# Ten instead of nine of the sixteen inner chunks in the first phase of a planned three-layer kernel

## The chip, the cores and the metric

One core of one Trainium2 chip runs the whole program. The metric is the device time of one execution in microseconds (us), as the median of several runs. The engines are PE (TensorE, the matmuls), DVE (VectorE), ACT (ScalarE), POOL (GpSimd) and SP (SyncE, which here issues all DMAs, the transposing ones too). Each engine takes its instructions strictly in the order in which they were written.

## The reference

Three layers follow each other: causal attention with a decay, a feed-forward layer with 2,048 inner features, and a second one with 1,024 inner features, a softmax gate and a layer norm.

```
# q, k, v: [4, 8, 576, 64], f: [4, 8, 576]
cum = cumsum(log(clip(f, 1e-4, 1)))
scores = q @ k.T / 8 + cum[:, None] - cum[None, :], causal
attn = softmax(scores) @ v                      # -> x: [2304, 512]
h = x @ w_in;  g = max(0.01 * h, h);  x = g @ w_out          # w_in [512, 2048]
h = x @ w2_in                                               # w2_in [512, 1024]
solu = h * softmax(h);  ln = layernorm(solu) * g_ln
out = ln @ w2_out                                           # [2304, 512]
```

## The kernel before

Every number is kept as a high and a low part (a split into two fp32r or fp16 tiles), so that each product takes three matmuls: high by high, high by low, low by high.

**Attention** goes by pairs of heads: 4 pairs for each of the 4 batches (`pair`). The first batch is done in two rounds, blocks 0 and 1 of all four pairs first, then blocks 2, 3 and 4; the other batches take whole pairs. A pair loads q and k into a `raw` tile (two of them), splits it into `kq` tiles on ACT, DVE and POOL, makes scores into `ps_s` (four PSUM banks), a softmax on ACT and DVE, a transposing DMA (`pt<-hl`), and the product with v into `ps_v` (one bank). Its result is spilled to DRAM (`xs_d`).

**The first feed-forward layer** goes by 9 blocks of 256 tokens. Its 16 chunks of 128 inner features are divided between two phases by the constant `FA`. In the first phase `ffn_a` does chunks 0 to `FA`-1 of every block: `load_x` fetches the block through two `xw` tiles into split `x` tiles, `hidden` makes a chunk (12 matmuls `ps_f<-x,wi`, two ACT and one DVE instruction into `g`), and `y_mms` adds up the output (12 matmuls `ps_f<-g,wo` a chunk); four partial outputs leave through `yo` tiles to DRAM (`yp_d`). These matmuls are woven into attention: blocks 0 and 1 can go when the first batch is spilled, blocks 2 and 3 after the second, 4 and 5 after the third. In the second phase `ffn_b` does the rest of the chunks (with `wib` and `wob`), adds the stored part, and `layer2` and `layer2_out` do the last layer.

**Weights** pass through `weight`: a load of 512 KB into a staging tile, a copy of the high halves into a `wk` tile (ACT or POOL), one DVE instruction (L798), a copy to the high part and a subtract into the low part. Up to `WI0` chunks of `wi` and `WO0` of `wo` are staged in three `wst` tiles, later ones in the two `raw` tiles that attention's loads use as well.

**Space** sets an order too. The tiles of the pool `early` (`wst`, `qa`, `vre`) lie where the pool `main` (`x`, `xw`, `g`, `yo`) comes later. So nothing of `main` can be written before the last weight that is staged in `wst` is done. The load of `glt` in `main` marks this place in SP's row.

**Order** is set by a planner (`Plan`): each operation has a priority and guessed durations, the planner plays a run through and writes out the instructions of each engine in the order that it finds. A changed count of operations or tiles so moves much else. `heirs` hands a tile on to another name when its first name needs it no more.

Of the kernel before, what the change touches and what calls it, by code (L numbers as in the profile page):

```python
# [7 lines left out]
F32 = mybir.dt.float32  # L8
# [4 lines left out]
BF16 = mybir.dt.bfloat16  # L13
AF = mybir.ActivationFunctionType
ALU = mybir.AluOpType
AX = mybir.AxisListType

B, H, S, D = 4, 8, 576, 64
# [3 lines left out]
KD = DM // 128  # L22
NC = DFF // 128
NC2 = DF2 // 128
FA = 9
PT = 4
NVT = 4
NWST = 3
NE = 2
EARLY = 1779.78  # L30
WI0 = 9
WO0 = 8
WLATE = 66.27
NVE = 1
# [23 lines left out]
TB = 256  # L58
# [271 lines left out]
def dve(n):  # L330
    return 1.042 * n + 70
# [18 lines left out]
def mmr(n):  # L350
    return n / 2.4 + 2.5 if n > 255 else 80.0
# [6 lines left out]
def body(tc, kqa, kq, vt, f, wa, w2i, w2o, gln, out):  # L358
    nc = tc.nc
    es = ExitStack()  # L360
    P = Plan()
# [3 lines left out]
    base = es.enter_context(tc.tile_pool(name="base", bufs=1))  # L365
# [3 lines left out]
    def tiles(pool, name, n, shape, dt):  # L369
        return [pool.tile(shape, dt, name=f"{name}{i}") for i in range(n)]  # L370


    P.tag("wi", tiles(base, "wi", FA, [128, 2, 512], F32R))
    P.tag("wo", tiles(base, "wo", FA, [128, 2, 512], F32R))
    P.tag("raw", tiles(base, "raw", 2, [128, KQ], F32))
    P.tag("wk", tiles(base, "wk", 2, [128, 512], I32))
    glt = base.tile([128, NC2], F32, name="glt")
    halfm = base.tile([128, 1], F32, name="halfm")
# [6 lines left out]
    ap = attn.enter_context(tc.tile_pool(name="attn", bufs=1))  # L385
# [1 line left out]
    P.tag("VT", tiles(ap, "VT", NVT, [128, 5, 2, 2, 64], F16))  # L387
    P.tag("u", tiles(ap, "u", 5, [128, 1], F32))
    P.tag("vs", tiles(ap, "vs", 2, [128, 4], I32))
    P.tag("sd", tiles(ap, "sd", 3, [128, S + 2], F32))  # L390
    P.tag("st", tiles(ap, "st", 6, [128, 12], F32))
    P.tag("hl", tiles(ap, "hl", 3, [128, 1536], F16))
    P.tag("pt", tiles(ap, "pt", PT, [128, 12, 128], F16))
    P.tag("xr", tiles(ap, "xr", 2, [128, S], F32))
    ident = ap.tile([128, 128], F32R, name="ident")
    P.tag("va", tiles(ap, "va", 2, [128, 1], F32R))
    mask = ap.tile([128, 512], BF16, name="mask")
    mask4 = ap.tile([128, S], BF16, name="mask4")
    zcol = ap.tile([32, 1], F32, name="zcol")
    zrow = zcol.to_broadcast([32, S])  # L400
    P.tag("qk", [tuple(ap.tile([128, KQ], F32R, name=f"kq{n}_{j}") for j in range(2)) for n in range(NQK)])
# [13 lines left out]
    def heirs(old, *plan):  # L415
        P.tags.setdefault(old, Tag(old)).heirs.extend(plan)
        for nm in plan:
            if not callable(nm):
                P.tags.setdefault(nm, Tag(nm))


    def copy_on(eng, o, i, scale=None):
# [50 lines left out]
    def setup():  # L473
        nc.gpsimd.memset(qa[64:66, 0], 1.0)
        nc.vector.memset(qa[64:66, 1], 1.0)
        nc.vector.memset(mask, 0.0)
        one_at = P.tags["sd"].free[-1][:, 0:128]
        nc.vector.memset(one_at, 0.0)
        nc.gpsimd.affine_select(
            one_at, one_at, pattern=[[-1, 128]], compare_op=ALU.not_equal, fill=1.0, base=0, channel_multiplier=1)  # L480
        nc.vector.tensor_copy(ident, one_at)
        nc.vector.memset(mask4, 0.0)
        nc.gpsimd.affine_select(
            mask[:, 384:512], mask[:, 384:512], pattern=[[-1, 128]], compare_op=ALU.is_ge,
            fill=NEG, base=0, channel_multiplier=1)
        for o in (0, 64):
            nc.gpsimd.affine_select(
                mask4[o:o + 64, 512:576], mask4[o:o + 64, 512:576], pattern=[[-1, 64]],
                compare_op=ALU.is_ge, fill=NEG, base=0, channel_multiplier=1)
        nc.gpsimd.memset(halfm, -0.5)  # L490
        for k in P.tags["wk"].free:
            nc.gpsimd.memset(k, 0)
        nc.vector.memset(zcol, 0.0)
# [131 lines left out]
    def qk_mm(Q, full, i, o, hd, k0, k1, first, last):  # L625
        _, qk, col = Q
        c0 = col[i]
        if full:
            a = qk(hd)
            mm(o, a[0:66, c0:c0 + 128], a[0:66, k0:k1], first, last)  # L630
            return
        a, b = qk(hd)
        mm(o, a[:, c0:c0 + 128], a[:, k0:k1], first, False)
        mm(o, b[0:68, c0:c0 + 128], b[0:68, k0:k1], False, last)
# [40 lines left out]
    def scores(p, unit, hd, prio, full):  # L675

        sts, parts, n, at = P.buf("st"), [], 0, 0
        for j, i in enumerate(unit):
            W = 128 * (i + 1)
            joint = i < 2 and len(unit) > 1  # L680
            if i == 1 and joint:
                at = 128
            else:
                ps, at = P.buf("ps_s"), 0
            view = lambda at=at, W=W, ps=ps: ps.t[:, at:at + W]
            key = (ps, j) if joint else ps
            P.op(PE, 4 * W / 2.4 if full else 2 * mmr(W), lambda Q=QK[p], i=i, W=W, view=view: qk_mm(
                Q, full, i, view(), hd, 0, W, True, True), prio, r=QK[p][0][hd], heat=HEAT if full else 1.0,
                **({"rw": [ps]} if at else {"w": [ps]}))
            parts.append([view, sts, j, W, [(n, n + W, 0, W)], key, i])  # L690
            n += 2 * W
        for view, _, j, W, _, key, i in parts:
            P.op(DVE, dve(W) + 130, lambda i=i, j=j, view=view: nc.vector.tensor_tensor_reduce(  # L693
                view(), view(), mask[:, 384 - 128 * i:512], -0.125, 3.0e38, ALU.add, ALU.min, sts.t[:, j:j + 1]),
                prio, w=[(sts, j)], rw=[key])
        parts = [x[:6] for x in parts]
        pt = softmax(parts, prio)
        return {i: (pt, x[4][0][0] // 128) for i, x in zip(unit, parts)}

    def scores4(p, prio, full):  # L700

        pa, pb, sts = P.buf("ps_s"), P.buf("ps_s"), P.buf("st")
        bq = QK[p][0]
        parts = []
        for ps, k0, k1, init in ((pa, 0, 512, 3.0e38), (pb, 512, S, None)):
            def pe(ps=ps, k0=k0, k1=k1, Q=QK[p]):
                for hd in range(2):
                    qk_mm(Q, full, 4, ps.t[:, 0:k1 - k0], hd, k0, k1, hd == 0, hd == 1)

            n = k1 - k0  # L710
            P.op(PE, 8 * n / 2.4 if full else 4 * mmr(n), pe, prio, w=[ps], r=bq[0] + bq[1], heat=HEAT if full else 1.0)
            P.op(DVE, dve(n) + 130, lambda ps=ps, k0=k0, k1=k1, n=n, init=init: nc.vector.tensor_tensor_reduce(
                ps.t[:, 0:n], ps.t[:, 0:n], mask4[:, k0:k1], -0.125, sts.t[:, 1:2] if init is None else init,
                ALU.add, ALU.min, sts.t[:, 0:1] if init is None else sts.t[:, 1:2]),
                prio, r=[(sts, 1)] if init is None else [], rw=[ps],
                w=[(sts, 0) if init is None else (sts, 1)])
            parts.append((lambda ps=ps, n=n: ps.t[:, 0:n], sts, 0, n,
                          [(0, 512, 0, 512)] if k0 == 0 else [(1024, 1088, 0, 64)], ps))
        return softmax(parts, prio)
# [125 lines left out]
    def y_mms(o, c, d, g, n, first, last):  # L845
        w = WO[c].t
        wh, wl = (w[:, j, 128 * d:128 * d + 128] for j in range(2))
        gh, gl = (g.t[:, j, 0:n] for j in range(2))
        mm(o, wh, gh, first, False)
        mm(o, wh, gl, False, False)  # L850
        mm(o, wl, gh, False, last)
# [23 lines left out]
    def ffn_a(blk, prio):  # L875
        eprio = prio - EP
        xb = load_x(blk, prio, "x")
        gs = [hidden(c, xb, TB, "ps_f", "g", prio + c, eprio + c) for c in range(FA)]
        YPD[blk] = []
        for d in range(KD):  # L880
            ps, yo = P.buf("ps_f"), P.buf("yo")
            for q in range(2):
                cs = range(FA // 2 * q, FA if q else FA // 2)

                def pe(cs=cs, d=d, ps=ps):
                    for c in cs:
                        y_mms(ps.t[:, 0:TB], c, d, gs[c], TB, c == 0, c == FA - 1)

# [5 lines left out]
    def ffn_b(tb, prio):  # L894
# [9 lines left out]
        at = [lambda: p01.t[:, 0:TB], lambda: p01.t[:, 512:512 + TB], lambda: p2.t[:, 0:TB], lambda: p3.t[:, 0:TB]]  # L904
        for c in range(FA, NC):
            g = hidden(c, xb, TB, "ps_g", "g2", prio + 2 * (c - FA), eprio + c)
# [100 lines left out]
    with tc.manual_schedule():  # L1007
# [6 lines left out]
        for p in range(KD):  # L1014
            pair(p, PB + PB0 * p, (2, 3, 4))
        for load_w, t, n, at in ((load_wi, "wi", WI0, WIP), (load_wo, "wo", WO0, WOP)):
            for c in range(FA):
# [6 lines left out]
        def main():  # L1024
            early.close()
            nc.sync.dma_start(glt, gln)
            mp = es.enter_context(tc.tile_pool(name="main", bufs=1, side="right"))
            P.tag("x", tiles(mp, "x", 8, [128, 2, TB], F32R))
            P.tag("xw", tiles(mp, "xw", 2, [128, 2, TB], F32))
            P.tag("g", tiles(mp, "g", FA, [128, 2, TB], F32R))  # L1030
            P.tag("yo", tiles(mp, "yo", 4, [128, TB], F32))

        P.op(CTL, 1.0, main, 0.0, deps=[o for o in P.ops if any(b.tag.name in ("wst", "qa", "vre") for b in o.bufs)])
        for blk in range(NB):
# [28 lines left out]
        for n in ("ps_f", "ps_g", "yo", "wst", "raw", "raw2", "wk"):  # L1063
            P.tags.setdefault(n, Tag(n)).fifo = False
        heirs("py01", "ph")
        heirs("raw", "raw2", "raw2")
        heirs("x", *(["x2"] * 4 + ["ln"] * 4))
        heirs("g", *(["g2"] * (FA - 5) + ["y2"] * 5))
        heirs("ps_f", "ps_g", "ps_g", "py3")
# [56 lines left out]
```

## Time and profile before

| what | value |
|---|---|
| median of 3 runs (lowest, highest) | 850.28 us (850.12, 850.7) |
| the profiled execution | 849.04 us |
| its span, first to last instruction | 847.2 us |
| mean granted TensorE clock | 0.98 |
| PE busy | 777.7 us (92%) |
| PE weight loads busy | 707.1 us (83%) |
| DVE, ACT, POOL busy | 523.0, 488.8, 364.5 us |

The shares are means over stages of different kinds: up to 98 us PE does attention alone, up to about 368 us attention with feed-forward matmuls between, and afterwards feed-forward work alone. The profiled execution lies 1.84 us over its span, and 1.24 us under the median.

### The profile page before, as it was taken

Reading aid. Unit: us, or ns where it says so; the run is one execution under the profiler, and the core shown is the slowest. Engines: PE = TensorE matmul, PEld = TensorE weight load, DVE = VectorE, ACT = ScalarE, POOL = GpSimd, SP = SyncE. Lnnn points to the kernel's source line nnn. Section 1 sums busy time; section 2 is a strip of 40 time slices with the busy share of each in tenths; the row PEclk is TensorE's granted clock in tenths of the full one; section 3 lists DMA queues with packets and bytes.
Section 4 is the critical chain, followed back from the end, with each engine's and each line's share of the span. In section 5 each row is a group of like instructions: output and inputs, shape, how many; then the busy total and the mean of one; then the engine's idle time right before and its main releaser. Section 6 shows DMA issues by size and latency. Waiting matters only on the chain.

```text
span 847.2 us, 15672 instructions
## 1 busy us (share of the span) xinstructions
PE 777.7 (92%) x5648; PEld 707.1 (83%) x5648; DVE 523.0 (62%) x1301; ACT 488.8 (58%) x1210; POOL 364.5 (43%) x433
## 2 busy tenths in 40 slices
PE   2477799987899999999999999999999999999997
PEld 2345689975798889999999998899889988998985
DVE  7899888887878788736544755334342434243641
ACT  5799798977988889736644533332433243324321
POOL 7888757546756474026311323322332233223321
PEclk9999899995899999999999999999999999999999
DMA  9799778787868786755554513321314131312113
GB/s 285 199 231 226 178 142 183 129 185 156 184 137 179 126 197 115 147 165 187 168 175 157 190 26 87 71 68 26 87 38 101 26 88 38 87 26 63 26 42 95
DMA packets 179757, 106.66 MB, mean 126 GB/s; under 512 B 146608, under 2 KB 162496, under 8 KB 179680
## 3 DMA queue, kind: packets, MB, share of 16 engines
q1 hardware_dynamic: 179680, 105.67, 52.3%
q8 instruction: 44, 0.72, 0.4%
q14 instruction: 33, 0.27, 0.1%
HBM read 55.72 MB, written 14.78 MB: 83 GB/s over the span
## 4 chain that ended last, share of the span: by engine, by line
PE 58%; DVE 4%; DMA 3%; ACT 3%; issue 1%; POOL 1%; DVEq 0%; SPq 0%; ACTq 0%; POOLq 0%
PE ps_f L470 36%; PE ph L470 11%; PE py L470 8%; DMA pt<-hl 2%; PE ps_s L470 1%; PE ps_v L470 1%; DMA tr<-hl 1%; ACT hl L424 1%; DVE hl L435 1%; DVE st L657 0%; ACT ps_s L643 0%; DVE g L841 0%; DVE raw L952 0%; DVE ps_s L693 0%; DVE s L944 0%
## 5 line engine op out<-in xcount | busy, mean ns | idle before, releaser
L470 PE MATMUL ps_f<-x,wi 128*128 128x256 f32 x972 | 129.6, 288 | 0.8 <-DVE g L841 0.8
L470 PEld LDWEIGHTS ps_f<-x,wi 128*128 128x128 f32 x972 | 123.6, 193 | 2.0 <-DVE g L841 1.2
L470 PE MATMUL ps_f<-g,wo 128*128 128x256 f32 x972 | 124.2, 283 | 1.2 <-DVE g L841 1.2
L470 PEld LDWEIGHTS ps_f<-g,wo 128*128 128x128 f32 x972 | 119.5, 188 | 1.8 <-DVE g L841 1.5
L470 PE MATMUL ps_s<-kq 128*128 128x512 f32 (+4 forms) x352 | 95.4, 396 | 25.8 <-DVE hl L435 22.4
L470 PE MATMUL ps_f<-x,wib 128*128 128x256 f32 x756 | 98.3, 281 | 0.7 <-DVE g L841 0.4
L470 PEld LDWEIGHTS ps_s<-kq 128*128 128x128 f32 x352 | 65.9, 226 | 39.2 <-DVE hl L435 22.2
L470 PE MATMUL ph<-wi,g 128*128 128x512 f32 x408 | 98.3, 396 | 0.0
L839 ACT ACTIVATE g<-ps_f 128x256 fp32r<-128x256 f32 x144 | 55.2, 383 | 71.9 <-PE ps_f L470 70.8
L470 PEld LDWEIGHTS ps_f<-x,wib 128*128 128x128 f32 x756 | 92.8, 188 | 1.8 <-DVE g L841 1.7
L470 PEld LDWEIGHTS ph<-wi,g 128*128 128x128 f32 x408 | 76.0, 188 | 17.6
L439 POOL TENSOR_TENSOR kq<-raw,kq 64x576 fp32r<-64x576 f32 (+2 forms) x55 | 82.6, 1502 | 14.6 <-ACT kq L424 9.2
L435 DVE SCALAR_TENSOR_TENSOR hl<-ps_s,st,hl 128x512 f16<-128x512 f32 (+4 forms) x160 | 82.2, 538 | 9.1 <-ACT hl L424 7.3
L643 ACT ACTIVATE ps_s<-ps_s,st 128x512 f32<-128x512 f32 (+4 forms) x160 | 78.8, 493 | 13.0 <-DVE st L693 7.7
L841 DVE TENSOR_TENSOR g<-ps_f,g 128x256 fp32r<-128x256 f32 x144 | 60.2, 420 | 41.0 <-ACT ps_f L840 39.3
L470 PE MATMUL ps_f<-wo,x 128*128 128x512 f32 x348 | 83.9, 396 | 0.0
L424 ACT ACTIVATE hl<-ps_s,st 128x512 f16<-128x512 f32 (+4 forms) x146 | 73.0, 538 | 12.3 <-issue 3.2
L470 PEld LDWEIGHTS ps_f<-wo,x 128*128 128x128 f32 x348 | 64.7, 188 | 14.9
L470 PE MATMUL ps_v<-pt,VT 128*128 128x128 f16 (+1 forms) x928 | 65.4, 234 | 12.7 <-DVE xr L728 4.3
L470 PE MATMUL py<-g,wob 128*128 128x256 f32 x567 | 76.6, 279 | 0.0
L470 PEld LDWEIGHTS <-VT 128*128 128x128 f16 x928 | 56.2, 110 | 22.8 <-issue 13.2
L470 PEld LDWEIGHTS py<-g,wob 128*128 128x128 f32 x567 | 72.4, 188 | 1.9
(152 smaller groups left out, 1198.5 us busy)
## 6 DMA issues: line engine op xcount, KB each, us to landing
wst<-wa SPq DMA_DIRECT2D x17, 512.0 KB
raw<-wa SPq DMA_DIRECT2D x15, 512.0 KB
raw<-kq SPq DMA_DIRECT2D x12, 608.0 KB
xw<-xs_d SPq DMA_DIRECT2D x24, 256.0 KB
yp_d<-yo SPq DMA_DIRECT2D x36, 128.0 KB
yw<-yp_d SPq DMA_DIRECT2D x18, 256.0 KB
out<-ot SPq DMA_DIRECT2D x18, 256.0 KB
vr<-vt SPq DMA_DIRECT2D x13, 320.0 KB
```

The costliest lines, as they stand in the source:

```text
L424: nc.scalar.activation(o, i, CP, scale=1.0 if scale is None else scale)
L435: nc.vector.scalar_tensor_tensor(o, a, scale, b, op0=ALU.mult, op1=ALU.subtract)
L439: (nc.vector if eng == DVE else nc.gpsimd).tensor_tensor(o, a, b, op=ALU.subtract)
L470: nc.tensor.matmul(o, lhsT=l, rhs=r, start=start, stop=stop)
L643: P.op(ACT, act(W, 1, True) + 93, lambda view=view, j=j, k=k: nc.scalar.activation(view(), view(), AF.Exp, bias=sts.t[:, j:j + 1], scale=- ...
L839: P.op(ACT, act(n, 0, True), lambda: nc.scalar.activation(g.t[:, 0, 0:n], h(), AF.Prelu, scale=WSC, alpha=0.01), eprio, w=[(g, 0)], r=[ps])
L841: P.op(DVE, dve(n) + 60, lambda: nc.vector.tensor_tensor(g.t[:, 1, 0:n], h(), g.t[:, 0, 0:n].bitcast(F32), op=ALU.subtract), eprio, w=[(g, ...
```

## The change

One more of the sixteen chunks is done in the first phase, so `FA` goes from 9 to 10, and `WI0` with it, so that the tenth `wi` is staged in `wst` as well; the tenth `wo` goes through `raw`. The first phase needs space for one `wi`, one `wo` and one `g` tile more. It comes from the three `sd` tiles of the cumulative sums, which are used at the start alone: they now live in the pool `base`, and are inherited afterwards, two as the `xw` tiles and one as two of the four `yo` tiles. The mask for the causal blocks grows by 128 columns, and the zeros of the other mask (`mask4`) are read from it.

```
-FA = 9
+FA = 10
...
-WI0 = 9
+WI0 = 10
...
+    P.tag("sd", tiles(base, "sd", 3, [128, S + 2], F32))
...
-    P.tag("sd", tiles(ap, "sd", 3, [128, S + 2], F32))
...
-    mask = ap.tile([128, 512], BF16, name="mask")
-    mask4 = ap.tile([128, S], BF16, name="mask4")
+    mask = ap.tile([128, 640], BF16, name="mask")
+    mask4 = ap.tile([128, 64], BF16, name="mask4")
...
+    pair_of = lambda t: t[:, 0:512].rearrange("p (a b) -> p a b", a=2)
+    heirs("sd", *[lambda t: [("xw", pair_of(t))]] * 2, lambda t: [("yo", t[:, 0:256]), ("yo", t[:, 256:512])])
...
-            mask[:, 384:512], mask[:, 384:512], pattern=[[-1, 128]], compare_op=ALU.is_ge,
+            mask[:, 512:640], mask[:, 512:640], pattern=[[-1, 128]], compare_op=ALU.is_ge,
...
-                view(), view(), mask[:, 384 - 128 * i:512], -0.125, 3.0e38, ALU.add, ALU.min, sts.t[:, j:j + 1]),
+                view(), view(), mask[:, 512 - 128 * i:640], -0.125, 3.0e38, ALU.add, ALU.min, sts.t[:, j:j + 1]),
...
-                ps.t[:, 0:n], ps.t[:, 0:n], mask4[:, k0:k1], -0.125, sts.t[:, 1:2] if init is None else init,
+                ps.t[:, 0:n], ps.t[:, 0:n], mask[:, 0:512] if init is not None else mask4, -0.125, sts.t[:, 1:2] if init is None else init,
...
-            P.tag("xw", tiles(mp, "xw", 2, [128, 2, TB], F32))
             P.tag("g", tiles(mp, "g", FA, [128, 2, TB], F32R))
-            P.tag("yo", tiles(mp, "yo", 4, [128, TB], F32))
+            P.tag("yo", tiles(mp, "yo", 2, [128, TB], F32))
```

The planner makes other orders of it. In SP's row the loads of block 0's x (`xw<-xs_d`) stood behind the load of `glt`, which is where the pool `main` opens. Before:

```order
L467 DMA_TRANSPOSE pt_131<-hl_126 128x6x128
L461 DMA vr_104<-vt 128x640
L461 DMA kq_1_143<-dr_d 4x1216
L1026 DMA glt<-gln 128x8
L461 DMA xw_862<-xs_d_87 128x2x256
L461 DMA xw_863<-xs_d_87 128x2x256
L467 DMA_TRANSPOSE pt_128<-hl_127 128x9x128
```

With the change the same loads go into two of the old `sd` tiles, and stand close behind the spill of the last pair that they read:

```order
L464 DMA xs_d_92<-xr_135 128x256
L464 DMA raw_84<-kq 128x960
L464 DMA wst_152<-wa 128x2048
L470 DMA_TRANSPOSE pt_133<-hl_129 128x8x128
L464 DMA sd_86<-xs_d_92 128x2x256
L464 DMA sd_85<-xs_d_92 128x2x256
L470 DMA_TRANSPOSE pt_130<-hl_127 128x6x128
```

So the x loads moved 19 rows up, and no longer behind the last weight that is staged in `wst`.

On POOL, the rows around the last `wst` weight (`wo_79` before, with 9 + 8 weights staged there) and the first x. Before:

```order
L439 TENSOR_TENSOR wo_79<-wst_150,wo_79 128x512
L439 TENSOR_TENSOR kq_1_141<-raw_82,kq_0_140 64x576
L657 TENSOR_SCALAR st_123<-st_123 128x1
L431 TENSOR_SCALAR x_854<-xw_862 128x256
L657 TENSOR_SCALAR st_119<-st_119 128x1
L439 TENSOR_TENSOR x_854<-xw_862,x_854 128x256
```

With the change (`wi_72` is the tenth `wi`, `wo_80` the last weight in `wst`; `wo_81` and `wo_82` are the ninth and tenth `wo`, each in a `raw` tile):

```order
L442 TENSOR_TENSOR wi_72<-wst_152,wi_72 128x512
L442 TENSOR_TENSOR wo_80<-wst_153,wo_80 128x512
L434 TENSOR_SCALAR x_854<-sd_86 128x256
L434 TENSOR_SCALAR x_856<-sd_85 128x256
L442 TENSOR_TENSOR x_854<-sd_86,x_854 128x256
L442 TENSOR_TENSOR x_855<-sd_86,x_855 128x256
L442 TENSOR_TENSOR x_857<-sd_85,x_857 128x256
L442 TENSOR_TENSOR kq_1_143<-raw_84,kq_0_142 64x576
L442 TENSOR_TENSOR kq_0_142<-raw_84,kq_0_142 64x384
L434 TENSOR_SCALAR wo_81<-raw_83 128x512
L442 TENSOR_TENSOR wo_81<-raw_83,wo_81 128x512
L434 TENSOR_SCALAR wk_89<-raw_84 128x512
```

The x work now follows the last `wst` weight at once, and two more weights stand around it.

On PE, the first chunk of block 2 (`ps_f<-x,wi`), after a stretch in which attention had PE for itself. Before it stood behind the scores `ps_s` of a further unit:

```order
L470 MATMUL ps_s_161<-kq_0_140 128x512
L470 MATMUL ps_s_161<-kq_1_141 128x512
L470 MATMUL ps_s_162<-kq_0_144 128x64
L470 MATMUL ps_s_162<-kq_1_145 128x64
L470 MATMUL ps_s_162<-kq_0_140 128x64
L470 MATMUL ps_s_162<-kq_1_141 128x64
L470 MATMUL ps_f_154<-x_854,wi_63 128x256 x3
L470 MATMUL ps_f_154<-x_855,wi_63 128x256 x3
```

With the change it stands 28 attention matmuls earlier, ahead of a product with v (`ps_v`, 64 columns) and those scores:

```order
L473 MATMUL ps_s_163<-kq_0_146 128x256
L473 MATMUL ps_s_163<-kq_1_147 128x256
L473 MATMUL ps_f_158<-x_854,wi_63 128x256 x3
L473 MATMUL ps_f_158<-x_855,wi_63 128x256 x3
L473 MATMUL ps_f_158<-x_856,wi_63 128x256 x3
L473 MATMUL ps_f_158<-x_857,wi_63 128x256 x3
L473 LDWEIGHTS VT_110
L473 MATMUL ps_v_166<-pt_132,VT_110 128x64
```

Counted over PE's whole row, the feed-forward matmuls that stand ahead of the last attention matmul are 1,188 of 4,320 before and 1,308 with the change; the last one of block 1 stands behind 574 attention matmuls in both, the very first one behind 258 before and 228 with the change, and the first one of block 2 behind 740 and 712.

## Rows read from the trace of the kernel before

**Rows 1.** Busy time by stage (x instructions): PE, PEld, DVE, ACT, POOL, then granted clock, DMA share.
```profile
0.00:84.00 84.00, 45.47 (x209) 32.94 (x209) 72.93 (x202) 67.75 (x160) 70.80 (x84) 1.00 0.88 235
84.00:98.00 14.00, 8.29 (x60) 6.80 (x60) 12.71 (x31) 9.99 (x25) 7.98 (x11) 0.97 0.82 184
98.00:184.00 86.00, 83.52 (x760) 80.08 (x760) 72.14 (x226) 77.39 (x211) 53.06 (x52) 0.96 0.78 158
184.00:218.00 34.00, 22.52 (x150) 18.60 (x148) 27.89 (x85) 24.89 (x64) 19.62 (x20) 0.68 0.78 170
224.00:368.00 144.00, 139.00 (x1308) 132.45 (x1309) 115.44 (x350) 122.75 (x342) 67.01 (x72) 1.00 0.73 146
368.00:459.00 91.00, 90.84 (x755) 90.47 (x755) 46.53 (x78) 47.11 (x110) 28.71 (x31) 1.00 0.57 184
459.00:816.00 357.00, 356.33 (x2274) 320.63 (x2273) 159.90 (x306) 126.60 (x275) 105.28 (x151) 1.00 0.27 67
```

**Rows 2.** The chain that ended last, in time: start, length, what.
```profile
366.90 1.13 PE ps_v L470 x20
368.03 13.02 PE ps_f L470 x108
```

**Rows 3.** The stages of Rows 1 for tile ps_f alone: PE, PEld, DVE, ACT.
```profile
224.00:368.00 144.00, 99.02 (x750) 93.69 (x751) 16.46 (x41) 31.01 (x84) 1.00 0.73 146
```

**Rows 4.** Timeline of SP's queue up to block 0's x loads: start, length, what.
```profile
62.31 4.28 SPq L467 DMA_TRANSPOSE pt<-hl  x2
...
68.05 1.02 SPq L461 DMA_DIRECT2D wst<-wa  x2
...
77.03 0.38 SPq L461 DMA_DIRECT2D wst<-wa  x1
...
77.87 0.34 SPq L461 DMA_DIRECT2D raw<-wa  x1
...
87.53 0.34 SPq L1026 DMA_DIRECT2D glt<-gln  x1
87.97 0.90 SPq L461 DMA_DIRECT2D xw<-xs_d  x2
...
94.47 0.39 SPq L461 DMA_DIRECT2D raw<-kq  x1
```

**Rows 5.** Timeline of POOL, ACT and PE: last staged weights, block 0's x, first feed-forward matmuls.
```profile
77.81 1.62 POOL L439 TENSOR_TENSOR wi<-wst,wi 128x512 fp32r<-128x512 f32 x1
...
85.94 1.29 POOL L439 TENSOR_TENSOR wo<-wst,wo 128x512 fp32r<-128x512 f32 x1
...
93.42 0.41 POOL L431 TENSOR_SCALAR x<-xw 128x256 fp32r<-128x256 f32 x1
95.35 3.24 POOL L439 TENSOR_TENSOR x<-xw,x 128x256 fp32r<-128x256 f32 x4
...
73.93 0.77 ACT L424 ACTIVATE wk<-wst 128x512 f16<-128x512 bf16 x1
82.15 0.79 ACT L424 ACTIVATE wk<-wst 128x512 f16<-128x512 bf16 x1
91.50 0.78 ACT L424 ACTIVATE wk<-raw 128x512 f16<-128x512 bf16 x1
...
98.08 2.91 PE L470 MATMUL ps_f<-x,wi 128*128 128x256 f32 x12
```

**Rows 6.** Timeline of PE around the stretch without feed-forward matmuls.
```profile
179.83 3.52 PE L470 MATMUL ps_f<-g,wo 128*128 128x256 f32 x28
...
212.56 1.05 PE L470 MATMUL ps_s<-kq 128*128 128x128 f32 x4
215.37 0.69 PE L470 MATMUL ps_v<-pt,VT 128*128 128x64 f16 x18 [1.76 <-DVE xr L728]
216.04 3.20 PE L470 MATMUL ps_s<-kq 128*128 128x384 f32 x10
219.05 2.91 PE L470 MATMUL ps_f<-x,wi 128*128 128x256 f32 x12
```

**Rows 7.** Timeline of SP's queue in the same stretch.
```profile
208.74 0.34 SPq L461 DMA_DIRECT2D xs_d<-xr  x1
209.33 3.49 SPq L467 DMA_TRANSPOSE pt<-hl  x2
212.88 2.13 SPq L461 DMA_DIRECT2D xw<-xs_d  x4
```

**Rows 8.** Groups by line: busy us, mean ns of one, idle before.
```profile
L839 ACT ACTIVATE g<-ps_f 128x256 fp32r<-128x256 f32 x144 | 55.2, 383 | 71.9 <-PE ps_f L470 70.8
L841 DVE TENSOR_TENSOR g<-ps_f,g 128x256 fp32r<-128x256 f32 x144 | 60.2, 420 | 41.0 <-ACT ps_f L840 39.3 <-PE ps_f L470 1.0
```

More of the change, by code (lines that the diff above doesn't have):

```diff
@@ L487, in setup @@
             nc.gpsimd.affine_select(
-                mask4[o:o + 64, 512:576], mask4[o:o + 64, 512:576], pattern=[[-1, 64]],
+                mask4[o:o + 64], mask4[o:o + 64], pattern=[[-1, 64]],
                 compare_op=ALU.is_ge, fill=NEG, base=0, channel_multiplier=1)
```

## The prediction

> **What bounds the kernel now.** I read the busy time by stage first [rows 1]. From 459 to 816 us PE is busy 356.3 of 357 us, from 368 to 459 us 90.84 of 91, and from 224 to 368 us 139.0 of 144: there the kernel is as long as PE's work. Before that PE has holes. Up to 84 us it is busy 45 of 84 us while DVE (73) and ACT (68) are near full: attention's start is theirs. From 98 to 184 us it is full again (83.5 of 86), and from 184 to 218 us it is busy 22.5 of 34 us at a granted clock of 0.68, so part of that time at the lower of its two levels (1.2 GHz). So PE's losses lie in two places: ahead of 98 us, and between 184 and 218 us.
>
> The timeline of PE says what these places are. The first full chunk of feed-forward work runs at 98.08 us [rows 5]; the last matmuls of blocks 0 and 1 end at 183.35 us, and the first chunk of block 2 runs at 219.05 us [rows 6]. Between these attention runs alone, because block 2 needs the second batch, whose last spill is issued at 208.74 us [rows 7]. The last attention matmul ends at 368.0 us, and from there PE only works off what is left [rows 2]. So I look for the end in two parts: when attention ends, and how many feed-forward matmuls then remain.
>
> **What remains after attention.** The number of matmuls is the same in both kernels. Counted in PE's row, 1,188 feed-forward matmuls stand ahead of the last one of attention before, and 1,308 with the change: 120 fewer remain. 108 of them took 13.02 us right after attention [rows 2], 0.1206 us each, so 120 x 0.1206 = 14.5 us less. PE has no room there in which they could hide, so this term is the firmest. The question is by how much the same 120 matmuls push the end of attention back.
>
> **The start of the feed-forward work.** Before, block 0's x loads stand behind the opening of the pool `main` and are issued at 87.97 us [rows 4], the first copy runs on POOL at 93.42 and the four subtracts end at 98.6 [rows 5]. The last staged weight was done at 85.94 + 1.29 = 87.2 us. So x came 11 us after its space. With the change the loads stand behind the transpose of 62.31 us, and x's copies follow the last staged weight directly. That weight comes later, since one more (the tenth `wi`) is staged before it: its load needs the `wst` tile that the ninth `wi` leaves; POOL's subtract of that one ran at 77.81 us, and stands about there in the new row too. From the issue of a load to the `wk` copy took 5.1 us (77.03 to 82.15) and 5.9 (68.05 to 73.93) [rows 4, 5], from that copy to the end of the subtract 5.1 (82.15 to 87.23): 78 + 5.3 + 5.1 = 88.5 us. Two copies of 0.41 and a subtract of 0.8 later PE can start, near 91 us: 7 us earlier. At the best the last weight is done no later than before, and PE starts at 89 (9 us). At the worst a load takes 13.6 us, as the `raw` load of 77.87 did till its copy at 91.50: 78 + 13.6 + 5.1 + 2 = 99, one us later than now. I take 91, since it was `wst` loads in the same stretch that took 5 to 6 us.
>
> **From there to the hole.** The last matmul of block 1 stands behind the same 574 attention matmuls in both. Ahead of it now come 48 more feed-forward matmuls (two blocks, 24 each; 48 x 0.1206 = 5.8 us) and the 30 attention matmuls that the earlier start leaves behind. An attention matmul costs (139.0 - 99.0) / (1308 - 750) = 0.072 us [rows 1, 3], so 2.1 us. PE is full in this stage (97%), so all of it counts: the hole begins at 183.3 - 7.1 + 7.9, some 0.8 us later than now. The extra chunk also gives ACT two instructions of 0.38 us a block and DVE one of 0.42 [rows 8], and the two weights give POOL, DVE and ACT work that they had later; ACT is busy 77 of 86 us here. I cost this at nothing, with PE as the cover. If that cover were gone, it would be 4 x 0.38 = 1.5 us on ACT.
>
> **The hole.** Before, block 2's first chunk stood behind 28 more attention matmuls, and ran at 219.05; with the change it stands where the scores of 212.56 us end [rows 6]. That would give up to 219.05 - 213.6 = 5.4 us, if x is there. x's loads were issued 4.1 us behind the spill, with two transposes between [rows 7]; now one stands there. So the loads can come 1 to 2 us earlier, though they must wait for the spill to land. I take 4 us (bounds 0 and 5.4). Then the first chunk of block 2 runs at 219.05 + 0.8 - 4 = 215.9 us.
>
> **From there to the end of attention.** 72 more feed-forward matmuls (8.7 us) and the 28 attention matmuls left behind (2.0 us) give 10.7. PE was idle 5.0 of 144 us here [rows 1]; I let 0.3 of the idle time fill up, since the planner weaves the additions evenly and most of those gaps are single waits. Attention ends 0.8 - 4 + 10.4 = 7.2 us later, at 375 us.
>
> One rule bears on this term. PE is busy 96.5% of the stage, its weight loads 132.45 of 144 us, 92% [rows 1]. The Trainium skill, "Perfetto Trace Analysis", section "Identifying the Most-Contended Engine", says that matmul busy time is no good measure of how near PE is to its limit, and that the busy share of the weight loads is a better one. By that measure 11.6 us are free in this stage, and the 10.7 us would fit in them; the result would be some 10 us lower than mine. The trace agrees where 256-column matmuls run alone (90.84 and 90.47 of 91 us), and disagrees from 459 to 816 us, where PE has no gaps and the loads are busy 320.6 of 357 us. I keep PE's own row in the sum.
>
> **The last phase.** One chunk less stands between the steps of the last layer there (24 matmuls, 2.9 us a block), with the same chains on DVE, ACT and POOL. DVE is busy 160 of 357 us [rows 1]. In the new row each output product still stands about as many matmuls behind its input product as before, so I put down 0.5 us (bounds 0 and 3).
>
> **The sum.** +7.2 for attention's end, -14.5 for what remains, +0.5: -6.8 us. From the profiled execution's 849.04 that is 842.2 us; the median of the runs stands 1.24 us over it, so the forecast is 843.5 us. The bounds of the terms (start -9 to +1, hole 0 to -5.4, last phase 0 to 3) put the likeliest case between 840 and 847.
>
> **The rivals.**
> *The start gains nothing.* The DMA engines are busy 88% of the first 84 us [rows 1], and the change puts one more 512 KB weight and block 0's loads of x into that time. If the last weight takes its worst time, PE starts at about 98 as now, and the sum is -6.8 + 7 = about 0: 850.5. For it: the one load that took 13.6 us. Against: the two `wst` loads around it took 5 to 6.
>
> *POOL waits for the tenth `wo`, and attention with it (slower).* Both `raw` tiles now hold a weight before the second batch's first q and k are loaded; before, one stayed free for it, and that load was issued at 94.47 us [rows 4]. In POOL's new row the `wk` copy of the tenth `wo` stands behind x and ahead of that batch's split. By the durations above it is reached near 96.5 us. If its load, issued near 89, needs the 13.6 us of the other `raw` load, POOL stands still to 102.6 us, and everything of attention behind it comes 6 us later and the second `raw` load with it; PE's row has its scores in order and cannot pass them. With a wait of more than 7 us the gain is gone; with 9 to 10 the time is 853. Against: attention's split in POOL has other work of some 2 to 5 us that is due only later.
>
> *PE has more room than its row shows.* By the weight loads (above), or because the earlier start also lets the clock rise sooner, the addition up to 368 us costs little. Half to all of 10.7 us would fit, for a time of 834 to 839, say 837.
>
> **How the numbers follow.** I give the forecast 0.62, the start without gain 0.14, POOL's wait 0.12, more room 0.12. A measurement of this kernel tells differences of some 0.2% (1.7 us) from nothing, so "faster" is below 848.6. The likeliest case is faster but for 0.02; of the case around 850.5 a quarter is faster, 0.6 the same and the rest slower. That makes 0.75 faster, 0.12 the same, 0.13 slower. The range from 836.5 to 851.5 holds nearly all of the likeliest case (0.59), most of the start's case (0.12), over half of the case with more room (0.07) and the near end of POOL's wait (0.03).
>
> **What the profile of the changed kernel would show.** The first chunk `ps_f<-x,wi` near 91 us; if near 98, the first step is wrong. The last spill of the second batch near 208 us and the first chunk of block 2 near 216, with a hole of about 32 us and a clock of 0.6 to 0.7 in it. The last `ps_v` near 375 us: at 382 all is lost, at 368 to 370 there was more room. From there to the end some 14 us less than the 479 us of now. The forecast is wrong if the stage from 98 us on is not full on PE any more, or if PE shows gaps behind 460 us where the last layer's chains are waited for.

## The result, and the profile after

The change took 855.21 us (median of 10 runs, 851.89 to 857.67) against 850.49 us of the kernel before on the same chip (10 runs, 848.18 to 853.04). The ratio is 1.0055, interval 1.0036 to 1.0074: 4.7 us slower, where 843.5 us and faster had been forecast. Its profiled execution spans 853.0 us, at a mean granted clock of 0.976.

The busy time by stage in the change, from the stage with the hole on; columns as in [rows 1], which these lines answer:

```profile
184.00:218.00 34.00, 21.99 (x143) 16.90 (x142) 29.20 (x86) 24.92 (x68) 17.89 (x17) 0.71 0.74 163
224.00:368.00 144.00, 138.34 (x1256) 133.24 (x1256) 112.06 (x348) 117.84 (x337) 71.93 (x74) 0.95 0.69 144
459.00:816.00 357.00, 352.54 (x2282) 317.88 (x2282) 167.06 (x311) 132.09 (x285) 114.07 (x163) 1.00 0.30 77
```

Two lines are new in kind. From 224 to 368 us PE did 1,256 matmuls where it did 1,308 before, and the clock there is 0.95 where it was 1.00: PE lost time in a stage that I had taken as full, although its busy time is nearly the same (138.34 and 139.00 us). The last 357 us also have 4.5 us without PE work, where there had been 0.7; but 3.4 of them are there without the cause found below as well (PE busy 353.60 in the first experiment).

The timeline of PE shows the marks of the prediction: the first feed-forward chunk, the end of block 1 (the `ps_f` work that ends at 187.7), the first chunk of block 2, and a gap that the kernel before doesn't have.

```profile
94.02 0.41 PE L473 MATMUL ps_f<-x,wi 128*128 128x256 f32 x1
...
185.65 2.04 PE L473 MATMUL ps_f<-g,wo 128*128 128x256 f32 x15
...
212.00 2.07 PE L473 MATMUL ps_s<-kq 128*128 128x512 f32 x6 [3.46 <-DVE hl L438]
...
219.84 1.20 PE L473 MATMUL ps_s<-kq 128*128 128x128 f32 x4
220.92 1.47 PE L473 MATMUL ps_f<-x,wi 128*128 128x256 f32 x4
...
308.01 3.74 PE L473 MATMUL ps_f<-g,wo 128*128 128x256 f32 x30
315.31 1.14 PE L473 MATMUL ps_v<-pt,VT 128*128 128x64 f16 x18 [3.56 <-DMA pt<-hl]
316.27 3.39 PE L473 MATMUL ps_s<-kq 128*128 128x384 f32 x10
...
325.05 1.29 PE L473 MATMUL ps_v<-pt,VT 128*128 128x128 f16 x20
```

At 315.31 PE had waited 3.56 us for a transpose. The timeline of SP's queue says what stood ahead of it:

```profile
214.91 5.97 SPq L464 DMA_DIRECT2D sd<-xs_d  x4
...
303.14 6.92 SPq L464 DMA_DIRECT2D sd<-xs_d  x4
310.11 1.81 SPq L464 DMA_DIRECT2D yp_d<-sd  x1
312.01 2.66 SPq L470 DMA_TRANSPOSE pt<-hl  x2
...
387.50 6.05 SPq L464 DMA_DIRECT2D sd<-xs_d  x4
```

These are the x loads of blocks 2, 4 and 6, the ones whose 256 tokens lie in two batches, so that each of the two tiles is loaded in two pieces. Before, the four loads took 2.13 us at block 2 [rows 7], and this at block 4:

```profile
293.91 2.56 SPq L461 DMA_DIRECT2D xw<-xs_d  x4
```

Now they hold the queue for 6 to 7 us. In the chain that ended last, at block 6 (start, length, what), the queue waits for a landing (the arrival of a load's data), issues, and waits again; the first line is the end of attention:

```profile
384.46 1.15 PE ps_v L473 x20
...
387.50 2.63 DMA sd<-xs_d
...
390.15 0.37 SPq L464
...
390.57 2.58 DMA sd<-xs_d
```

Each second piece waits until the first piece of the same tile has landed. The order of SP's row with its semaphores (the counters by which one instruction waits for another) says so. At block 2, before:

```
149 L461 DMA xw0_862<-xs_d0_87 128x2x64 [waits DMAHW6_49]
150 L461 DMA xw0_862<-xs_d1_88 128x2x192 [waits DMAHW7_49]
151 L461 DMA xw1_863<-xs_d0_87 128x2x64 [waits DMAHW0_49]
152 L461 DMA xw1_863<-xs_d1_88 128x2x192 [waits DMAHW3_49,DMAHW1_49]
```

and with the change, where the second and the fourth wait for one semaphore more, that of the load just ahead (`DMAHW6`, `DMAHW0`):

```
149 L464 DMA sd1_86<-xs_d0_92 128x2x64
150 L464 DMA sd1_86<-xs_d1_93 128x2x192 [waits DMAHW7_49,DMAHW6_49]
151 L464 DMA sd0_85<-xs_d0_92 128x2x64 [waits DMAHW0_49]
152 L464 DMA sd0_85<-xs_d1_93 128x2x192 [waits DMAHW3_49,DMAHW1_49,DMAHW0_49]
```

The two pieces write different columns, so nothing in the data asks for this. Before, an `xw` tile was allotted as `[128, 2, 256]`. Now it is the first 512 columns of a tile of 578, seen as 2 x 256 through `rearrange`, and the program that sets the semaphores puts a wait between the two column ranges of that view. By what rule it compares them was not looked into; that the view is what brings the wait is shown by the experiments. The waits of SP's queue over the whole run (us in total, times, longest) have a line that the kernel before lacks:

```profile
SPq L464 <- DMA sd<-xs_d: 25.7, 12, 3.3
```

Twelve waits: two at each of three blocks, in both phases. ACT and POOL are held up too, since x's copies stand in their rows among the softmax's work (POOL waits 2.79 us for x at 309.37). ACT's timeline at block 4:

```profile
312.90 0.72 ACT L427 ACTIVATE x<-sd 128x256 fp32r<-128x256 f32 x2 [2.44 <-DMA sd<-xs_d]
```

### The profile page after: what moved, and what is told of

Its sections match the earlier page's. It is cut to its first block, busy times and chain, and to the rows that moved or that the text cites. A ratio compares the mean times of both kernels' runs of the same rounds, so it can differ in the third digit from the quotient of the medians.

```text
span 853.0 us, 15674 instructions
## 1 busy us (share of the span) xinstructions
PE 776.3 (91%) x5648; PEld 706.9 (83%) x5648; DVE 520.7 (61%) x1295; ACT 479.7 (56%) x1206; POOL 373.8 (44%) x445
## 4 chain that ended last, share of the span: by engine, by line
PE 47%; DMA 7%; DVE 5%; ACT 4%; POOL 2%; issue 2%; SPq 0%; DVEq 0%; POOLq 0%; ACTq 0%
PE ps_f L473 30%; PE ph L473 10%; PE py L473 4%; DMA sd<-xs_d 3%; DMA tr<-hl 3%; PE ps_s L473 1%; PE ps_v L473 1%; ACT hl L427 1%; DMA raw<-w2o 1%; POOL hl L442 1%; DVE raw L972 1%; ACT raw L949 1%; ACT ps_s L646 1%; DVE g L442 0%; DVE raw L955 0%
## 5 line engine op out<-in xcount | busy, mean ns | idle before, releaser
L473 PE MATMUL ps_f<-x,wi 128*128 128x256 f32 x1080 | 145.7, 290 | 2.8 <-DVE g L844 1.6
L473 PEld LDWEIGHTS ps_f<-x,wi 128*128 128x128 f32 x1080 | 137.8, 194 | 5.1 <-DVE g L844 1.9
L473 PE MATMUL ps_f<-g,wo 128*128 128x256 f32 x1080 | 139.1, 286 | 0.0
L473 PEld LDWEIGHTS ps_f<-g,wo 128*128 128x128 f32 x1080 | 133.7, 191 | 0.1
L438 DVE SCALAR_TENSOR_TENSOR hl<-ps_s,st,hl 128x384 f16<-128x384 f32 (+4 forms) x160 | 82.3, 539 | 12.1 <-ACT hl L427 10.9
L473 PE MATMUL ps_f<-x,wib 128*128 128x256 f32 x648 | 83.1, 279 | 0.3 <-DVE g L844 0.2
L442 POOL TENSOR_TENSOR kq<-raw,kq 64x576 fp32r<-64x576 f32 (+2 forms) x51 | 78.1, 1534 | 6.7 <-ACT kq L427 3.7
L473 PEld LDWEIGHTS ps_f<-x,wib 128*128 128x128 f32 x648 | 78.5, 188 | 0.7 <-DVE g L844 0.7
L696 DVE CUSTOM_DVE_ANT_0 ps_s<-ps_s,mask 128x128 f32<-128x128 f32 (+3 forms) x128 | 62.3, 495 | 10.9 <-PE ps_s L473 10.0
L473 PE MATMUL py<-g,wob 128*128 128x256 f32 x486 | 64.4, 277 | 0.0
```

The lines of the kernel that those rows point to most:

```text
L438: nc.vector.scalar_tensor_tensor(o, a, scale, b, op0=ALU.mult, op1=ALU.subtract)
L442: (nc.vector if eng == DVE else nc.gpsimd).tensor_tensor(o, a, b, op=ALU.subtract)
L473: nc.tensor.matmul(o, lhsT=l, rhs=r, start=start, stop=stop)
```

## The experiments

**Theory A**: the wait between the two pieces is what makes the change slower; the tenth chunk by itself is a gain, as forecast. **Theory B**: the chunk itself or its place costs the time (attention has no room for 120 more matmuls ahead of its end), and the wait is hidden. Four kernels (e1 to e4), with the change itself, cross the two: with or without the chunk, with or without the wait. In the first of them (e1) the tile is allotted so that its plain slice is the `xw` view, and the instructions stand in the same order as in the change:

```
-    P.tag("sd", tiles(base, "sd", 3, [128, S + 2], F32))
+    P.tag("sd", tiles(base, "sd", 3, [128, 2, S // 2 + 1], F32))
+    wide3 = {}
+    for i, t in enumerate(P.tags["sd"].free):
+        P.tags["sd"].free[i] = u = t.rearrange("p a b -> p (a b)")
+        wide3[id(u)] = t
...
-    pair_of = lambda t: t[:, 0:512].rearrange("p (a b) -> p a b", a=2)
+    pair_of = lambda t: wide3[id(t)][:, :, 0:TB]
```

> The change, with the old sd tiles allotted as [128, 2, 289] and not as [128, 578], so that the two pieces of an x load that spans two batches no longer wait for each other; every instruction stands where it stands in the change. Theory A (the loss is this wait: SP is held for about 6 us instead of 2 at blocks 2, 4 and 6, and the transposes behind it are late): the four loads take 2 to 3 us of SP's queue, the hole of PE near 308 to 320 us and its half clock go, the last attention matmul ends near 377 instead of 385.6, and the median is 845 to 849. Theory B (the extra chunk delays attention by its own work and place in the rows): 854 to 856, the hole near 310 us stays.

Measured: 844.46 us (6 runs), 0.9922 of before (0.9901 to 0.9944). Its span is 842.9 us. It beats the kernel before as well as the change, and lies just below the 845 to 849 that I had expected. SP's queue and PE at block 4:

```profile
300.73 2.01 SPq L468 DMA_DIRECT2D sd<-xs_d  x4
...
305.60 3.74 PE L477 MATMUL ps_f<-g,wo 128*128 128x256 f32 x30
309.18 0.70 PE L477 MATMUL ps_v<-pt,VT 128*128 128x64 f16 x18
309.72 1.99 PE L477 MATMUL ps_s<-kq 128*128 128x384 f32 x10
...
314.86 1.29 PE L477 MATMUL ps_v<-pt,VT 128*128 128x128 f16 x20
```

The four loads take 2.01 us, and the `ps_v` of 309.18 follows on PE without a gap.

The wait alone, put into the kernel before, in the same order of instructions (e2):

```
-            P.tag("xw", tiles(mp, "xw", 2, [128, 2, TB], F32))
+            P.tag("xw", [t[:, 0:2 * TB].rearrange("p (a b) -> p a b", a=2) for t in tiles(mp, "xw", 2, [128, S + 2], F32)])
```

> The kernel before, with its two xw tiles as views of tiles that are 578 wide, which makes the same wait between the pieces of an x load; all else stands as before. Theory A: 4 to 9 us slower than before (854 to 859), with the loads near 294 us taking about 6 us of SP's queue instead of 2.6, and a hole of PE behind them. Theory B: as before within 1.5 us.

Measured: 860.03 us (857.16 to 861.08), 1.0103 (1.0079 to 1.0126). The same 12 waits appear, as many us long as in the change:

```profile
SPq L461 <- DMA xw<-xs_d: 25.8, 12, 2.8
```

PE's gap at block 4 is there too, but it ends in another way than in the change. ACT stands 2.69 and 1.43 us at x's copies for a landing, the softmax comes behind them in its row, and PE waits 3.20 us for the softmax; no transpose is on this path:

```profile
304.99 0.72 ACT L424 ACTIVATE x<-xw 128x256 fp32r<-128x256 f32 x2 [1.43 <-DMA xw<-xs_d]
...
307.63 2.60 PE L470 MATMUL ps_s<-kq 128*128 128x384 f32 x6 [3.20 <-DVE hl L435]
```

The kernel before waited 1.62 us at this place:

```profile
305.00 1.74 PE L470 MATMUL ps_s<-kq 128*128 128x384 f32 x6 [1.62 <-DVE hl L435]
```

The space without the chunk, with the wait (e3: `FA = 9` and `WI0 = 9` in the change):

> The change with 9 chunks again, so the shared tiles and masks alone, the piece wait with them. Theory A: slower than before, 853 to 859. Theory B (the chunk is the loss): as before, 849 to 852, since no chunk is added.

Measured: 857.46 us (855.54 to 860.18), 1.0086 (1.006 to 1.0113). At block 4 PE waits 4.49 us for the softmax, and ACT for x, as in e2.

The space without the chunk and without the wait (e4: the same two constants in the first experiment's kernel):

> The shared tiles and masks with 9 chunks, without the piece wait. Theory A: as before or up to 3 us faster, since the x loads of block 0 come earlier (847 to 851); its distance to the first of these runs is what the tenth chunk alone is worth. Theory B: as before, 849 to 852, and the first run of these four is 4 to 6 us slower than this one.

Measured: 850.32 us (846.89 to 852.41), 0.9989 (0.997 to 1.0007).

So the wait costs 9.3 us in the old kernel (860.03 - 850.72, the median of before on that chip), 7.1 without the chunk (857.46 - 850.32) and more with it (below). The chunk is worth 850.32 - 844.46 = 5.9 us where there is no wait, and the space with its early x loads nothing. With the wait the chunk is worth some 2 us of 850 (1.0086 less 1.0063, the mean ratio of the change's two samples), so the wait and the chunk do not simply add up. B falls, A stands.

**Where the wait costs.** Next the wait is put back into the first experiment's kernel at one place at a time (e5 to e8, in this order). `flatv` holds the flat view of each tile, and the condition stands for the place (block 2; block 4; block 6; `tag == "x2"`):

```
+        xt = (lambda xw: flatv[id(xw.t)][1]) if (tag == "x" and blk == 2) else (lambda xw: xw.t)
...
-                load((xw, at), lambda xw=xw, o=at - t0, n=n: xw.t[:, :, o:o + n],
+                load((xw, at), lambda xw=xw, o=at - t0, n=n: xt(xw)[:, :, o:o + n],
```

In all four every instruction stands where it stood; only the waits of these loads differ.

> The kernel e1_no_piece_wait with the wait put back at one place alone: the loads of block 2's x in the first phase. Same order of all instructions. A (each place costs what the traces of the change and of e1 show there): attention stood 2.4 us later in the change than in e1 from the 522nd ps_v on (233.2 against 230.3 us), so 844.5 + 2.4 = 846.9; the four loads near 215 us hold SP some 6 us instead of 1.6. B (the places don't add up: later work takes the delay in, and the cost comes from one place or only from all together): 844.5, as in e1.

> The kernel e1_no_piece_wait with the wait at block 4's x in the first phase alone. A: this is the dear place. Between the 696th and the 754th ps_v the change took 28.9 us and e1 21.1, of which the next ones gave back some 2.6: 5.2 to 7.8 us, so 849.7 to 852.3; PE stands near 310 us for pt, and the four loads near 301 us hold SP 6 to 7 us instead of 2. B: 844.5, the gap then needs the delay of block 2 as well.

> The kernel e1_no_piece_wait with the wait at block 6's x in the first phase alone. Its loads are issued when attention has ended, so no transpose of attention is held up behind them. A: 0 to 1.5 us (PE had a gap of 1.09 us near 406 us in the change), 844.5 to 846. B: 844.5. Were the late x itself the cost, and not what stands behind it on SP, it would be here as dear as at block 4.

> The kernel e1_no_piece_wait with the wait at the spanning blocks of the second phase alone (x2 of blocks 2, 4 and 6). There the transposes of the last layer stand behind the loads on SP. From the end of attention to the end the change took 2.5 us more than e1, of which block 6 has its part. A: 1 to 2.5 us, 845.5 to 847. B: 844.5.

Measured on one chip (before 849.28 us there): block 2 alone 848.99 us, ratio 0.9991 (0.9974 to 1.0008); block 4 alone 848.1, 0.9985 (0.9971 to 0.9998); block 6 alone 846.88, 0.9968 (0.9953 to 0.9983); the second phase alone 842.94, 0.9931 (0.9916 to 0.9946). Without the wait the ratio was 0.9922, and 0.9916 in a second sample below. From their mean, 0.9919, the prices are 6.1, 5.6, 4.2 and 1.0 us of 850. Each is uncertain by some 2 us, so the second phase's is not told from nothing. Block 2 was expected to cost 2.4 us; the two times in that expectation (233.2 and 230.3) differ by 2.9, and 2.4 is what was left of this at 308 us.

Block 4 was dear as expected, with nearly the same gap on PE as the change (3.26 us). Block 6 cost 4 us where I had put 0 to 1.5. Its PE timeline has two gaps that e1's lacks (a second profile of e1's kernel has one of 0.77 us there):

```profile
392.88 4.85 PE L483 MATMUL ps_f<-x,wi 128*128 128x256 f32 x36
399.42 6.02 PE L483 MATMUL ps_f<-x,wi 128*128 128x256 f32 x48 [1.68 <-DVE g L854]
406.66 4.57 PE L483 MATMUL ps_f<-x,wi 128*128 128x256 f32 x36 [1.22 <-DVE g L854]
```

and the chain that ended last reaches them through what stands behind these x loads on SP, here the loads of the second phase's weights:

```profile
386.71 0.43 SPq L474
...
387.19 6.78 DMA raw<-wa
...
393.99 0.81 ACT wk L437
```

My expectation had named only transposes as what can be held up there. These weights were issued 1.1 us later than in e1 (386.71 for 385.63) and landed 3.0 us later, by the start of ACT's first copy (392.69 for 389.71); what made the landing longer is not shown. By the last sentence of the expectation a cost as at block 4 speaks for the late x as a cost of its own, and 4.2 and 5.6 us cannot be told apart.

**How long the queue is held.** The last four kernels (e9 to e12) ran on one chip. The first exchanges the two middle loads of a spanning block in the first phase of the change, so that the two landings pass side by side; nothing else moves:

```
+                if two and (q, i) == (0, 1):
+                    todo = []
+                elif two and (q, i) == (1, 0):
+                    todo = [(1, o, n), (0, cut, TB - cut)]
```

> The change with the wait left in, but with the two middle loads of blocks 2, 4 and 6 exchanged in the first phase: first piece of tile A, first piece of tile B, second piece of A, second piece of B. Each second piece still waits for its first piece, but the two landings now pass side by side, so SP should be held some 4 us instead of 6 to 7 (2 to 2.6 without any wait). Nothing else moves. A (the time for which these loads hold SP's queue is the cost): about half of the change's loss of 10.7 comes back, 848 to 851, and the gap of PE near 312 us shrinks to 1 or 2 us. B (x's late landing at the copies is the cost, whatever stands behind on SP): the last piece lands only some 2 us sooner, so 852 to 854.

> The kernel of e1_no_piece_wait once more, for a base on the same chip as the two kernels beside it: 0.992 of before (0.990 to 0.994), so some 843 to 845.

> The kernel of e5_wait_block2 once more, beside its base. Its first profile had attention end 0.5 us later than in e1 and a span only 0.8 us longer, but its median stood 0.7 per cent above that of e1 against before. A (the wait at block 2 costs 2.4 us): 846 to 847.5, 2 to 3 us above e10. B (it costs 6 us): 849 to 850. C (it costs nothing): as e10.

> The change itself, beside e1's kernel on the same chip, so that the whole price of the waits is read from one chip. A: 9 to 12 us above e10 and 0.4 to 0.7 per cent above before. Were the price of e1 against the change partly a matter of different chips, it would be under 8.

Measured (before 850.71 us there): without the wait 842.94 us, 0.9916 (0.9892 to 0.9939); the wait at block 2 alone 846.4, 0.9955 (0.9935 to 0.9974); loads exchanged 848.29, 0.9985 (0.9962 to 1.0007); the change 856.44, 1.007 (1.0041 to 1.0099). On one chip the wait thus costs the change 13.5 us, more than the 9 to 12 that I had expected, and block 2 alone 3.5 us, which is less than in its first sample. By the ratio, against 0.9919, block 2 costs 3.1 us here, and with the first 6.1 the mean is 4.6; the four single places then add up to 15 us, and the whole to 12.2 (by the mean ratio 1.0063 less 0.9919), which their uncertainties cover.

At block 2 the loss is plain in these two traces (e10 and e11). Without the wait the first chunk of block 2 runs in one piece (in e1 it had one wait of 0.50 us for x), and with it in three, with waits for x; the `ps_v` a little later stands at 228.99 and 232.10 us:

```profile
220.97 2.27 PE L477 MATMUL ps_f<-x,wi 128*128 128x256 f32 x12
...
228.99 1.28 PE L477 MATMUL ps_v<-pt,VT 128*128 128x128 f16 x20 [0.68 <-DMA pt<-hl]
```

```profile
220.59 1.47 PE L483 MATMUL ps_f<-x,wi 128*128 128x256 f32 x4
222.74 1.50 PE L483 MATMUL ps_f<-x,wi 128*128 128x256 f32 x3 [0.68 <-DVE x L452]
224.51 1.43 PE L483 MATMUL ps_f<-x,wi 128*128 128x256 f32 x5 [0.27 <-POOL x L452]
...
232.10 1.29 PE L483 MATMUL ps_v<-pt,VT 128*128 128x128 f16 x20
```

With the exchanged loads, SP and PE at block 4 read:

```profile
303.32 4.82 SPq L865 DMA_DIRECT2D sd<-xs_d  x4
...
313.42 0.70 PE L473 MATMUL ps_v<-pt,VT 128*128 128x64 f16 x18 [1.49 <-DMA pt<-hl]
313.95 2.07 PE L473 MATMUL ps_s<-kq 128*128 128x384 f32 x10
```

The queue is held 4.82 us instead of 6.92, PE's gap is 1.49 us instead of 3.56, and 8.2 of the 13.5 us come back. That speaks for the time in which SP is held. It does not prove it apart from the late x, since this edit shortens both; a kernel that delays x without holding SP wasn't tried. The traces show the wait reaching PE by both ways: at block 4 of the change the gap ends with a transpose that stood behind these loads on SP, and in e2 and e3 with a softmax that stood behind x's copies on ACT. How the price divides between the two stays open.

## Why the prediction was wrong

**The step that failed** is the cost of the x loads, which I took over from the kernel before in "The hole" and in "From there to the end of attention" without a term of their own. I looked at when they are issued and asked whether the spill has landed; I did not ask what the second load of a tile waits for once the tile is a view of a wider one. The four lines of SP's row were there to be read in the order with its waits. The runs showed in its place twelve waits, 25.7 us of SP's queue, and a price of 13.5 us on one chip (12.2 by the mean ratios). No rival had this either; the rival in which POOL waits for the tenth `wo` came close in time (853) by another mechanism.

**The rest of the sum came out near.** Without the wait the change runs at 0.9919 of before, the mean of two samples. That is 843.4 us of the shown 850.28, against 843.5 forecast, and inside the range. That the two agree to 0.1 us is luck in part: the profiled spans differ by -4.3 us (847.2 to 842.9; -3.1 in the second sample, 844.1), where the sum had -6.8. Its terms follow, up to the hole from the profile of the change, and behind it from that of e1, since there the wait spoils the change's own:

*The start of the feed-forward work*: 94.02 us, not 91. The mechanism was right, x follows the last staged weight at once, but that weight was done at 92.9 us, not at 88.5. SP and POOL in the change:

```profile
64.84 1.38 SPq L464 DMA_DIRECT2D sd<-xs_d  x2
66.61 3.70 SPq L470 DMA_TRANSPOSE pt<-hl  x2
70.36 0.57 SPq L464 DMA_DIRECT2D wst<-wa  x1
...
80.99 1.29 POOL L442 TENSOR_TENSOR wi<-wst,wi 128x512 fp32r<-128x512 f32 x1
...
91.61 1.29 POOL L442 TENSOR_TENSOR wo<-wst,wo 128x512 fp32r<-128x512 f32 x1 [1.32 <-ACT wo L427]
92.99 0.96 POOL L434 TENSOR_SCALAR x<-sd 128x256 fp32r<-128x256 f32 x2
```

I had begun my chain at 78, which is where the subtract of the ninth `wi` began; the tile is free when it ends, at 79.4 [rows 5], so 1.4 us were lost in the reading. In the change it ends at 82.3, 2.9 us later still. The early x loads are a part of that at most: SP issued the `wst` load ahead of them at 62.78 for 61.55, 1.2 us late already, and the one behind them at 70.36 for 68.05 [rows 4], 2.3 us late. From the end of that subtract to the last weight it took 10.6 us for a forecast 10.4, and PE began 1.1 us behind it, not 2.5. The tenth weight alone does not set the start: without it (e4) POOL's copies of x began 1.7 us earlier, at 91.32, and the first chunk ran at 94.09 all the same, behind attention matmuls.

*From there to the hole*: 93.7 us long (94.0 to 187.7) against 85.3, so +8.4 for a predicted +7.9. Right.

*The hole*: 33.2 us (187.7 to 220.9) against 35.7, so -2.5, not -4; and without the wait it ends no earlier (220.94 in e1, 220.97 in e10). Not x but the attention left in it, which waits for the softmax (3.46 us at 212.00, shown above), sets when it ends: the first chunk follows the scores of 219.84 without a gap. With the start this put the first chunk 5 us later than forecast.

*From there to the end of attention*: forecast +10.4. Without the wait it was 157.0 us (220.9 to 377.9) against 149.0, +8.0, so PE had a little more room than I gave it. With the wait it was 164.7 us, +15.7, and attention ended at 385.6, past the 382 that the prediction had as the mark of a lost gain. The difference is the wait at block 4 and what is left of that at block 2.

*What remains after attention and the last phase*: forecast -14.5 + 0.5 = -14.0. Without the wait -14.2 (842.9 - 377.9 = 465.0 against 479.2). Right to 0.2 us, and to 0.7 in the second sample (844.1 - 378.2 = 465.9). Its two parts were not measured apart: from 459 to 816 us PE stands 3.4 us even without the wait, where it stood 0.7, which is more than the 0.5 for the last phase. With the wait the whole is 467.4.

Together these terms miss by 3.0 + 0.5 + 1.5 - 2.4 - 0.2 = 2.4 us, which is the distance from -6.8 to -4.3 but for rounding.

The Trainium skill's measure by weight loads ("Perfetto Trace Analysis", section "Identifying the Most-Contended Engine") would have had the 10.7 us of that term fit into the gaps; 8.0 of 10.4 did show, so PE's own row was the nearer guide. The Trainium skill, "DMA: Bandwidth & Descriptors", section "Anatomy of one DMA — SWDGE (gpsimd) path", states that a wait on a semaphore happens in the sequencer that issues, before the DMA engines see anything. Here that is seen on SP, though the section is on another queue: landings of 2.58 and 2.63 us in the chain, and 25.7 us in all in which SP issued nothing else.

## What to carry to other kernels

When a tile becomes a view of another one, compare the order with its semaphores before and after, for each load that fills it in more than one piece: a wait on the load just ahead is a dependence that the data don't need, and allotting the tile in the shape of the view took it away. In a queue that issues in order, such a wait makes late not its own data alone but everything that stands behind it; here four loads of 0.4 us each held transposes and weight loads for 4 to 5 us more at each of three blocks in the first phase. The late data in turn hold up what stands behind their copies on other engines. The waits turned a gain of 0.8% into a loss of 0.6%. Price a moved transfer by what it waits for and what waits behind it, not by its old length.

## What the runs showed of the hardware that was not expected

The loss at block 4 was more than PE's gap. From the `ps_f` work of 308.01 to the `ps_v` of 325.05 the change took 17.0 us, and e1, in the same order, 9.3 (305.60 to 314.86): 7.8 us for a gap of 3.56. At the end of attention 5.3 of them are left (7.7 us late there, 2.4 at 308). After the gap of 3.56 us the granted clock of PE was near its lower level (1.2 of 2.4 GHz), while with the exchanged loads, after a gap of 1.49 us, it stayed at full. The stretch from 314 to 325 us in the change and then in the kernel with the exchanged loads (columns of [rows 1]):

```profile
314.00:325.00 11.00, 9.69 (x55) 9.30 (x55) 7.33 (x21) 7.23 (x22) 6.84 (x9) 0.53 0.77 169
```

```profile
314.00:325.00 11.00, 10.49 (x91) 9.53 (x87) 9.42 (x25) 9.53 (x31) 8.11 (x9) 1.00 0.76 172
```

PE was busy 9.69 and 10.49 of 11 us, but did 55 matmuls in the one and 91 in the other. The ten `ps_s` matmuls behind the gap took 3.39 us against 2.07. So in this stretch shortening a wait gave back more than its length.

The length of a gap does not settle what the clock does behind it. The kernel without the wait was profiled twice (e1, then e10), and a little later PE stood for a transpose nearly equally long in both. The 24 matmuls behind took 3.13 us in the one and 4.61 in the other, where the granted clock from 326 to 332 us was 1.00 and 0.72:

```profile
328.55 0.70 PE L477 MATMUL ps_v<-pt,VT 128*128 128x64 f16 x18 [2.22 <-DMA pt<-hl]
329.08 3.13 PE L477 MATMUL ps_f<-x,wi 128*128 128x256 f32 x24
```

```profile
327.37 0.70 PE L477 MATMUL ps_v<-pt,VT 128*128 128x64 f16 x18 [2.24 <-DMA pt<-hl]
327.90 4.61 PE L477 MATMUL ps_f<-x,wi 128*128 128x256 f32 x24
```

So one profile of a kernel does not price a gap of some 2 us; the same kernel can pay for it at the lower clock or not.
